# The last output tile of a fused retention and feed-forward kernel, closed one weight tile sooner and finished by column halves

## The chip, the core and the metric

The kernel runs on one core of a Trainium2 chip. The metric is the device time of one execution in microseconds (us); the kernel before takes 848.39 us, the median of 3 runs. TensorE (PE in the rows) multiplies matrices, ScalarE (ACT) and VectorE (DVE) work element by element, GpSimd (POOL) helps them, and SyncE (SP) does nothing but issue transfers. Transfers are carried by 16 DMA engines, whoever issues them; here the queues of SyncE (SPq, queue q1) and of ScalarE (ACTq, queue q10) issue.

## The reference

Eight batch entries, eight heads, 576 positions, head size 64. Retention (attention without softmax, with a decay), then a two-layer feed-forward net over the 4608 tokens:

```
scores = q @ k.T / sqrt(64)
x = (scores * decay(gamma_h, position difference >= 0)) @ v      # per batch entry and head
x = x as [4608, 512]                                             # token = 576 * batch + position
h = x @ w_in                                                     # w_in  512 x 2048
out = (h - tanh(h)) @ w_out                                      # w_out 2048 x 512
```

## The kernel before

The 576 positions are cut into nine chunks (`NC`, numbered 0 to 8) of 64 (`C`). One chunk of all eight batch entries makes a block of 512 tokens. For each block the hidden layer is made in 16 tiles (`NF`) of 128 rows, and the second product adds those 16 tiles up into four output tiles `t` of 128 tokens by 512 columns: tile `t` holds batch entries `2t` and `2t + 1`, 64 positions each. The four sums stand in four PSUM banks (`ops[n][t]`, tags o0 to o3).

Float32 is multiplied as a sum of three products of shortened words. Each hidden tile is held as a high part and a low part (`gs[n, f]`), each weight tile `wout[f]` likewise (index `a`), and the three products are high·high, high·low and low·high. So each output tile is the sum of 16 x 3 = 48 products of 128x128 by 128x512; the hidden tile is the stationary operand, which is loaded before every product, and the weight tile moves past it.

The order is written out by hand: every engine keeps the order of the program. The last block (`n` = 8, `NC - 1`) ends in one call of `mm2`, for the hidden tiles 14 and 15 together (`f - 1` and `f`). Its `groups` list says in which order (which of the two tiles, which output tile) are taken, three products each, 24 products in all. When a tile's sum is closed, `store_last` copies it out of PSUM into its quarter of one tile in SBUF (`obs[n][:, t]`): tiles 0, 2 and 3 on ScalarE (line 615), tile 1 on VectorE (line 613). Two transfers of 128 KB carry it to HBM (line 618), one for each batch entry: 64 rows of 2 KB, contiguous in HBM. The first of the two goes out on SyncE's queue and the second on ScalarE's (on SyncE's too for tile 0). Nothing follows but the end of the program (line 1322), where SyncE waits for every transfer to have landed and the engines meet.

Two more PSUM banks (tag "h", two buffers) hold scores and hidden tiles earlier on; nothing has written them since the last attention step, which is over at this point. VectorE has no more to do there than the copy of tile 1.

Of the kernel before, what the change touches and what calls it, by code (L numbers as in the profile page):

```python
# [9 lines left out]
F32 = mybir.dt.float32  # L10
# [4 lines left out]
ALU = mybir.AluOpType  # L15
# [3 lines left out]
NT, DM, DF = B * S, H * D, 2048  # L19
P = 128  # L20
NF = DF // P
NCC = DM // P
C = 64
NC = S // C
BLK = B * C
# [73 lines left out]
def retention_ffn(ctx: ExitStack, tc: tile.TileContext, ins, out, spill, wvar):  # L99
    nc = tc.nc  # L100
# [4 lines left out]
    psp = ctx.enter_context(tc.tile_pool(name="psp", bufs=1, space=PSUM))  # L105
# [6 lines left out]
    win, wout, wraw, masks = {}, {}, {}, {}  # L112
# [24 lines left out]
    halves = (slice(0, DM // 2), slice(DM // 2, DM))  # L137
# [367 lines left out]
    gs, ops, homes, obs = {}, {}, {}, {}  # L505
# [55 lines left out]
    def mm2(n, f, at=-1, between=None):  # L561
        first, final = (turn[0], turn[-1]) if n == 1 else (0, NF - 1)
        if f == first:
            ops[n] = [psp.tile([P, DM], F32, tag=f"o{t}", bufs=1, name=f"o{n}_{t}") for t in range(4)]
        if f != final:
            order = [(f, t, k) for k in range(3) for t in range(4)]
        elif n < NC - 1:
            order = [(f, t, k) for t in range(4) for k in range(3)]
        else:

            groups = [(0, 0), (0, 1), (1, 0), (1, 1), (0, 2), (1, 2), (0, 3), (1, 3)]
            order = [(f - 1 + s, t, k) for s, t in groups for k in range(3)]
        for place_, (f_, t, k) in enumerate(order):
            if place_ == at:
                between()
            g, a = [(gs[n, f_][0], 0), (gs[n, f_][0], 1), (gs[n, f_][1], 0)][k]
            nc.tensor.matmul(  # L577
                ops[n][t], g[:, t * P : (t + 1) * P], wout[f_][:, a, :],
                start=(f_ == first and k == 0), stop=(f_ == final and k == 2),
            )  # L580
            if (k, t) == (1, 2):
                middle = tc.nc.cur_bb.bb.instructions[-1].name
            if f_ == final and k == 2:
                (store_last if n == NC - 1 else store)(n, t)
        return middle

    def store(n, t):
# [150 lines left out]
    for j in range(B - 1):  # L738
# [8 lines left out]
        o = psp.tile([P, 8, C], F32, tag=("o2", "o3", "own")[j % 3], bufs=1, name=f"own_first{j}")[:, :4]  # L747
# [61 lines left out]
    first = 2 * B  # L809
# [100 lines left out]
    for k, (n, f) in enumerate(late):  # L910
        if k in (3, 16, 29):
            follow, scale = entry3(first + (0, 2, 5)[(3, 16, 29).index(k)], rest)
        if 0 < k < len(late) - 1:
            words(*late[k + 1])
        if k < len(late) - 2:
            resume(*late[k + 2])
        for ahead in (4, 5) if k == 0 else (5,):
            if k + ahead < len(late):
                fetch(*late[k + ahead])
        if k in (3, 16, 29):  # L920

            follow()
        if k in (6, 19):
            scale()
        if k in (7, 20):
            load_part(rest[0], 0)
        if k in (10, 23):
            prep(rest.pop(), 0)
        for _ in range(2 if k < 4 else 1):
            step()  # L930
        for _ in range((k > 5) + (19 < k < 26)):
            next(summed)
        if k < len(late) - 1:
            mm2(n, f)
        for _ in range({0: 3, 1: 3, 2: 3, 3: 2}.get(k, 4 < k < 16 or 21 < k < 24)):
            raw_words(*raws.pop(0))
# [258 lines left out]
    def stage_b(n, m0):  # L1195

        fetch(n, 3)
        for f in range(NF):
# [20 lines left out]
            if (n, f) != (NC - 1, NF - 2):  # L1219
                middle = mm2(n, f, later or -1, turn_)  # L1220
# [10 lines left out]
    for f in range(NF):  # L1231
        mm1(2, f)
        if f == 0:
            mm2(*late[-1])
        if f == 1:
            scale()
        for _ in range(2):
            next(summed, None)
        if f == 2:
            load_turn(2, 0)  # L1240
        if f == 6:
            prep_turn(2, 0)
            load_turn(1, 0)
            load_turn(1, 1)
        if f in (9, 10):
            prep_turn(1, f - 9)
        if 10 < f < 14:
            fetch(2, f - 11)
        if f > 13:
            split(2, f - 14, fetched.pop((2, f - 14)), False)  # L1250
# [75 lines left out]
```

## Time and profile before

| | |
|---|---|
| runs | 848.39 us (median of 847.99, 848.39, 848.69) |
| the profiled execution's own time | 849.77 us |
| its span, first to last instruction | 848.0 us |
| busy, share of the span | PE 99%, PE weight load 82%, DVE 57%, ACT 43%, POOL 10% |
| transfers | 174.95 MB, mean 206 GB/s |

The span is that of the instructions on the core; the 1.8 us between the span and the execution's own time lie around it. The busy share of TensorE includes the time in which a product drains through the array while the next one streams, so 99% says that it never stands still for long.

### The profile page before, as it was taken

The numbers are of one execution on the slowest core, as the hardware profiler recorded it, in microseconds if no ns is written. First come the engines' busy times: TensorE is split into PE (matmuls) and PEld (weight loads), VectorE is DVE, ScalarE is ACT, GpSimd is POOL, SyncE is SP. The second block draws the span as 40 slices with busy tenths as digits, with TensorE's granted clock in tenths as the row PEclk, the third lists the DMA queues.
The fourth block names the chain that finished last, engine by engine and source line by source line (L and its number), as shares of the span: only waits on it lengthen the run. The fifth ranks groups of instructions, "written<-read, shape, count | busy, mean of one in ns | idle before, by whom it ended". The sixth has DMA issues, their size and how long they took to land.

```text
span 848.0 us, 18635 instructions
## 1 busy us (share of the span) xinstructions
PE 840.1 (99%) x7694; PEld 694.0 (82%) x7694; DVE 483.4 (57%) x824; ACT 362.6 (43%) x732; POOL 82.5 (10%) x68
## 2 busy tenths in 40 slices
PE   8999999999999999999999999999999999999998
PEld 7788888888888888888888888888888888888886
DVE  5989878787567675344346755434456554443321
ACT  5887765454335454223244543322245532232321
POOL 0110002020000002111110001212100021121100
PEclk9999999999999999999999999999999999999999
DMA  9977978884787788444477665534677364452542
GB/s 342 321 293 225 371 232 300 243 280 132 224 272 271 228 308 249 149 153 170 132 236 224 209 181 194 187 125 170 207 214 209 108 201 171 133 191 75 147 115 62
DMA packets 71380, 174.95 MB, mean 206 GB/s; under 512 B 8704, under 2 KB 10368, under 8 KB 66048
## 3 DMA queue, kind: packets, MB, share of 16 engines
q1 hardware_dynamic: 70768, 172.85, 62.1%
q8 instruction: 60, 0.98, 0.5%
q10 hardware_dynamic: 528, 0.92, 0.3%
q14 instruction: 24, 0.20, 0.1%
HBM read 124.72 MB, written 48.76 MB: 205 GB/s over the span
## 4 chain that ended last, share of the span: by engine, by line
PE 97%; DVE 1%; ACT 1%; DMA 1%; issue 0%
PE o L577 32%; PE o L1136 15%; PE h L520 15%; PE pnew L1105 7%; PE pv L1105 7%; PE pown L1105 4%; PE py L1105 4%; PE pz L1105 4%; PE s L357 3%; PE new L357 2%; PE own L357 2%; DMA a<-in_first_dram 1%; PE wps L628 1%; ACT th L1155 0%; PE s_first L357 0%; PE new_first L357 0%
## 5 line engine op out<-in xcount | busy, mean ns | idle before, releaser
L577 PE MATMUL o<-wo,gh 128*128 128x512 f32 x608 | 156.0, 393 | 0.0
L577 PEld LDWEIGHTS o<-wo,gh 128*128 128x128 f32 x608 | 112.6, 188 | 24.6 <-DVE ob L599 0.4
L1159 POOL TENSOR_TENSOR c<-c,th 128x512 f32<-128x512 f32 x48 | 62.0, 1295 | 517.8 <-ACT th L1155 399.5
L1155 ACT ACTIVATE th<-c 128x512 f32<-128x512 f32 x72 | 45.5, 632 | 148.6 <-DVE c L1169 97.4
L520 PE MATMUL h<-xh,wi 128*128 128x512 f32 x384 | 98.1, 392 | 0.8 <-ACT wi L198 0.6
L520 PEld LDWEIGHTS h<-xh,wi 128*128 128x128 f32 x384 | 71.3, 188 | 17.0 <-ACT wi L198 1.1
L577 PE MATMUL o<-wo,gl 128*128 128x512 f32 x304 | 84.2, 389 | 0.0
L1136 PE MATMUL o<-wo,gs 128*128 128x512 f32 x288 | 70.6, 389 | 0.0
L577 PEld LDWEIGHTS o<-wo,gl 128*128 128x128 f32 x304 | 57.1, 188 | 11.9
L1136 PEld LDWEIGHTS o<-wo,gs 128*128 128x128 f32 x288 | 54.1, 188 | 11.2
L1105 PE MATMUL pnew<-xhv,ws 128*128 128x512 f32 x192 | 59.5, 391 | 0.3
L577 PE MATMUL o<-wo,gs 128*128 128x512 f32 x240 | 59.5, 394 | 0.0
L1105 PE MATMUL pv<-xhv,ws 128*128 128x512 f32 x192 | 59.1, 389 | 0.0
L357 PE MATMUL own<-qk,state 64*64 64x64 f32 x896 | 55.2, 221 | 0.0
L1165 DVE TENSOR_TENSOR work<-pown,work 128x512 f32<-128x512 f32 x24 | 16.6, 690 | 66.6 <-PE pown L1105 66.6
L357 PE MATMUL own<-qk,vr 64*64 64x64 f32 x928 | 54.0, 218 | 0.4 <-issue 0.4
L577 PEld LDWEIGHTS o<-wo,gs 128*128 128x128 f32 x240 | 44.4, 188 | 9.5
L520 PE MATMUL h<-xl,wi 128*128 128x512 f32 x192 | 52.1, 390 | 0.0
L1136 PE MATMUL o<-wo,gh 128*128 128x512 f32 x192 | 48.9, 389 | 0.0
L357 PEld LDWEIGHTS own<-qk,vr 64*64 64x64 f32 x928 | 45.1, 135 | 0.5 <-issue 0.5
L357 PEld LDWEIGHTS own<-qk,state 64*64 64x64 f32 x896 | 44.7, 135 | 0.0
L1121 DVE TENSOR_TENSOR gl<-s,gh 128x512 fp32r<-128x512 f32 x44 | 30.0, 688 | 23.5 <-PE o L577 13.2
(162 smaller groups left out, 1520.7 us busy)
## 6 DMA issues: line engine op xcount, KB each, us to landing
ws<-wvar_dram SPq DMA_DIRECT2D x41, 1024.0 KB, 4.9
s<-spill_dram SPq DMA_DIRECT2D x94, 256.0 KB, 4.2
qk<-in_qkv_dram SPq DMA_DIRECT2D x29, 512.0 KB, 4.8
vr<-in_qkv_dram SPq DMA_DIRECT2D x29, 512.0 KB, 4.9
spill_dram<-c SPq DMA_DIRECT2D x48, 256.0 KB, 2.6
spill_dram<-g SPq DMA_DIRECT2D x36, 256.0 KB, 3.5
rwi<-in_w_in_dram SPq DMA_DIRECT2D x16, 512.0 KB, 6.5
rwo<-in_w_out_dram SPq DMA_DIRECT2D x16, 512.0 KB, 5.4
```

The lines of the kernel that those rows point to most:

```text
L357: nc.tensor.matmul(out_, w, x, start=start, stop=stop)
L520: nc.tensor.matmul(hp, win[f][:, cc // 2, a, cc % 2 * P : (cc % 2 + 1) * P], x[:, cc, :], start=(k == 0), stop=(k == 3 * NCC - 1))
L577: nc.tensor.matmul(ops[n][t], g[:, t * P : (t + 1) * P], wout[f_][:, a, :], start=(f_ == first and k == 0), stop=(f_ == final and k == 2),)
L628: nc.tensor.matmul(wps[:, :cols], warm[:, :P], warm[:, :cols], start=True, stop=True)
L1105: nc.tensor.matmul(into, w[:, a, k], x[:, k], start=start and i == 0, stop=i == len(terms) - 1, skip_group_check=not start,)
L1121: nc.vector.tensor_tensor(gl, g, gh.bitcast(F32), op=ALU.subtract)
L1136: nc.tensor.matmul(ops[n][t], g[:, t * P : (t + 1) * P], wout[f][:, a, :], start=(j == 0 and f == fs[0] and k == 0), stop=last_,)
L1155: nc.scalar.activation(th, c, AF.Tanh)
L1159: nc.gpsimd.tensor_tensor(c, c, tanh(c), op=ALU.subtract)
L1165: nc.vector.tensor_tensor(u2, y, u2, op=ALU.add)
```

## The change

Of the last block, output tile 3 takes its products with hidden tile 14 before tile 2 takes its own, and its sum in bank o3 is closed there, one weight tile short; VectorE copies it into `obs[n][:, 3]`. The last three products of tile 3 (those with hidden tile 15) come at the very end, after tile 2 is closed and stored, in two column halves of 256, each into a bank of tag "h". VectorE adds each half to the copy in place, and each half is stored at once by a single transfer over both batch entries: the left half from SyncE's queue, the right one from ScalarE's.

```diff
-            groups = [(0, 0), (0, 1), (1, 0), (1, 1), (0, 2), (1, 2), (0, 3), (1, 3)]
+            groups = [(0, 0), (0, 1), (1, 0), (1, 1), (0, 3), (0, 2), (1, 2)]
             order = [(f - 1 + s, t, k) for s, t in groups for k in range(3)]
...
             nc.tensor.matmul(
                 ops[n][t], g[:, t * P : (t + 1) * P], wout[f_][:, a, :],
-                start=(f_ == first and k == 0), stop=(f_ == final and k == 2),
+                start=(f_ == first and k == 0), stop=(f_ == (final - 1 if n == NC - 1 and t == 3 else final) and k == 2),
             )
...
             if f_ == final and k == 2:
                 (store_last if n == NC - 1 else store)(n, t)
+            if f == final and n == NC - 1 and t == 3 and k == 2:
+                nc.vector.tensor_copy(obs[n][:, t], ops[n][t])
+        if f == final and n == NC - 1:
+            ob = obs[n][:, 3]
+            for queue, cols in zip((nc.sync, nc.scalar), halves):
+                o = psp.tile([P, BLK], F32, tag="h", bufs=2, name=f"o{n}_3_{cols.stop}")[:, : DM // 2]
+                for k, (part, a) in enumerate(((0, 0), (0, 1), (1, 0))):
+                    nc.tensor.matmul(o, gs[n, f][part][:, 3 * P :], wout[f][:, a, cols], start=(k == 0), stop=(k == 2))
+                nc.vector.tensor_tensor(ob[:, cols], o, ob[:, cols], op=ALU.add)
+                queue.dma_start(out[6:8, n * C : (n + 1) * C, cols], ob[:, cols])
```

## Rows read from the trace of the kernel before

**Rows 1.** The first page of the profile: the span, and TensorE's busy time, share of the span and instructions; and the chain of work that ended last, by engine.

```profile
span 848.0 us, 18635 instructions
PE 840.1 (99%) x7694; PEld 694.0 (82%) x7694; DVE 483.4 (57%) x824; ACT 362.6 (43%) x732; POOL 82.5 (10%) x68
...
PE 97%; DVE 1%; ACT 1%; DMA 1%; issue 0%
```

**Rows 2.** The chain that ended last, in order of time, from 820 us on: start, us, what.

```profile
819.78 24.04 PE o L577 x106
843.82 0.02 issue
843.85 0.58 ACT ob L615
```

**Rows 3.** The timeline of the end of the kernel: start us, us, engine, line, operation, out<-in, count; in brackets the idle time before and who ended it. Eight products in a row are shown first, then parts of the last 24.

```profile
835.49 1.98 PE L577 MATMUL o<-wo,gh 128*128 128x512 f32 x8
...
838.21 1.52 PE L577 MATMUL o<-wo,gs 128*128 128x512 f32 x6
...
841.13 0.69 DVE L613 COPY ob<-o 128x512 f32<-128x512 f32 x1 [4.69 <-PE o L577]
...
842.49 0.59 ACT L615 COPY ob<-o 128x512 f32<-128x512 f32 x1 [1.45 <-PE o L577]
...
843.10 0.50 ACTq L618 DMA_DIRECT2D out_dram<-ob  x1
...
843.42 0.39 PE L577 MATMUL o<-wo,gl 128*128 128x512 f32 x1
843.85 0.58 ACT L615 COPY ob<-o 128x512 f32<-128x512 f32 x1 [0.77 <-PE o L577]
844.46 0.50 ACTq L618 DMA_DIRECT2D out_dram<-ob  x1
```

**Rows 4.** The groups of instructions by line and shape, of the whole execution: count | busy us, mean ns of one | idle before. A product of 128x512, its weight load, VectorE's copy of tile 1, and an operation of VectorE on 256 columns with one operand in PSUM (`s_first`).

```profile
L577 PE MATMUL o<-wo,gl 128*128 128x512 f32 x304 | 84.2, 389 | 0.0
...
L577 PEld LDWEIGHTS o<-wo,gl 128*128 128x128 f32 x304 | 57.1, 188 | 11.9
...
L365 DVE TENSOR_TENSOR pm<-s_first,decay 128x256 f32<-128x256 f32 x7 | 2.9, 421 | 7.4 <-PE s_first L357 7.4
...
L613 DVE COPY ob<-o 128x512 f32<-128x512 f32 x1 | 0.7, 692 | 4.7 <-PE o L577 4.7
```

**Rows 5.** The issues of line 618: duration of one in ns (least, median, most), first and last start.

```profile
L618 SPq DMA_DIRECT2D out_dram<-ob x5: 466/472/597, 841.1 to 844.5; - x5
L618 ACTq DMA_DIRECT2D out_dram<-ob x3: 497/498/541, 841.9 to 844.5; - x3
```

**Rows 6.** The transfers between 838 and 848 us: packets by size (the "under" counts add up from the smallest), by queue, and issues with KB each and median us from issue to landing. These are the eight stores of the last block and nothing else.

```profile
DMA packets 640, 1.05 MB, mean 105 GB/s; under 512 B 128, under 2 KB 128, under 8 KB 640
...
q1 hardware_dynamic: 400, 0.66, 25.8%
q10 hardware_dynamic: 240, 0.39, 14.8%
...
out_dram<-ob SPq DMA_DIRECT2D x5, 128.0 KB, 2.3
out_dram<-ob ACTq DMA_DIRECT2D x3, 128.0 KB, 2.8
```

**Rows 7.** The same view of the issues between 844.44 and 844.47 us, the last two of the kernel.

```profile
out_dram<-ob SPq DMA_DIRECT2D x1, 128.0 KB, 2.3
out_dram<-ob ACTq DMA_DIRECT2D x1, 128.0 KB, 2.6
```

**Rows 8.** Stretches of the end of the kernel: busy time of the engines, then the granted clock, the mean busy share of the 16 DMA engines, and GB/s.

```profile
842.00:842.10 0.10, 0.10 (x2) 0.06 (x2) 0.00 (x0) 0.00 (x0) 0.00 (x0) 1.00 0.00 0
842.10:842.20 0.10, 0.10 (x2) 0.10 (x1) 0.00 (x0) 0.00 (x0) 0.00 (x0) 1.00 0.37 82
843.00:844.00 1.00, 0.81 (x4) 0.35 (x2) 0.00 (x0) 0.23 (x2) 0.00 (x0) 1.00 0.97 193
844.00:845.00 1.00, 0.00 (x0) 0.00 (x0) 0.00 (x0) 0.43 (x1) 0.00 (x0) 1.00 0.97 297
845.40:845.50 0.10, 0.00 (x0) 0.00 (x0) 0.00 (x0) 0.00 (x0) 0.00 (x0) 1.00 0.27 82
846.40:846.50 0.10, 0.00 (x0) 0.00 (x0) 0.00 (x0) 0.00 (x0) 0.00 (x0) 1.00 0.90 348
846.60:846.70 0.10, 0.00 (x0) 0.00 (x0) 0.00 (x0) 0.00 (x0) 0.00 (x0) 1.00 0.16 41
846.70:846.80 0.10, 0.00 (x0) 0.00 (x0) 0.00 (x0) 0.00 (x0) 0.00 (x0) 0.98 0.01 0
```

**Rows 9.** The transfers between 237.1 and 237.4 us: packets by size, and the queue with its packets, MB and share of 16 engines. In this stretch the packets are nearly all those of one load of a table (line 250), whose 128 rows are of 1 KB.

```profile
DMA packets 123, 0.12 MB, mean 396 GB/s; under 512 B 14, under 2 KB 116, under 8 KB 123
...
q1 hardware_dynamic: 123, 0.12, 126.5%
```

**Rows 10.** What SyncE's queue waited for between 835 and 849 us: us in total, times, longest.

```profile
SPq L1322 <- DMA out_dram<-ob: 1.9, 2, 1.0
```

## Prediction

> **What bounds the kernel now.** The page comes first: TensorE is busy for 99% of the span and makes 97% of the chain that ended last [rows 1]. So the body of the kernel is TensorE's, and the change takes nothing out of it: 24 products of 512 columns become 21 of 512 and 6 of 256, the same columns. What is at stake is the stretch behind the last product. The chain shows it as TensorE until 843.82, then ScalarE's copy of tile 3 until 844.43 [rows 2]; the timeline adds the two issues at 844.46 [rows 3]. There the instructions stop, but the span goes on for 3.5 us. The stretches show why: the transfers of the last tile move until 846.7 [rows 8], SyncE waits for their landing at the end of the program [rows 10], and the landing of the later one is 2.6 us after its issue [rows 7], at 847.06. The remaining 0.92 us to the end of the span, 847.98, is the closing of the program and stays. So the end is set by: last sum, copy or add, issue, transfer, landing.
>
> **The change part by part.**
>
> *Products.* Eight products take 1.98 us and one by itself 0.389 [rows 3, 4], so one follows the other after (1.98 - 0.39) / 7 = 0.227 us. The last 24 begin at 838.21 [rows 3]; number 21 begins at 842.74 and ends at 843.13, which now closes tile 2. The half products begin at 842.97. No 128x256 product of this type is in the trace. From below its pitch is half of 0.227 = 0.114; from above it is the weight load of 0.188 [rows 4], since the load is not halved. I take 0.12, near the lower end, because even with loads before each product the products of 512 columns go at their own pitch, so loads hide. The left half is then closed at 842.97 + 2 x 0.12 + 0.276 = 843.49 (at 0.188: 843.62) and the right one at 843.85 (at 0.188: 844.19). TensorE ends where it did, 843.81, or up to 0.4 later.
>
> *Copy of tile 3.* It is 0.69 us on VectorE [rows 4], from 841.82, when VectorE has finished with tile 1 [rows 3], to 842.51. VectorE has nothing else to do before 843.5, so it costs nothing; if VectorE were late, the left add would wait for it, with a reserve of 1 us. The banks "h" are free; no wait is added on TensorE.
>
> *Tile 2.* Closed by product 21 instead of 18, its copy starts 0.68 later, at 843.17 instead of 842.49 [rows 3], and its two transfers are issued at 843.78 instead of 843.10.
>
> *Adds.* 256 columns with an operand in PSUM took 0.42 [rows 4]: left 843.52 to 843.94, right 843.95 to 844.37. Before, the copy ended at 844.43. Removing that copy and adding in halves so gains 0.06.
>
> *Issues.* Queued ahead of the left half on SyncE is tile 2's first transfer, 843.78 to 844.25 (0.47 each [rows 5]); the left half is issued at 844.25. On ScalarE tile 2's second ends at 844.28, and the right half is issued at 844.40. Before, both were issued at 844.46. Gain at the later issue: 0.06 (with the slower products a loss of 0.3).
>
> *The transfers themselves.* This is the term that decides. Each store before moves 64 rows of 2 KB. The eight stores have 640 packets, of which 128 are small [rows 6]: for each store 64 of data and 16 small closing ones, one for each of 16 engines, so each engine takes four rows; the outermost count of both sides is 64. The new stores are the first of another shape: the destination `out[6:8, 64 positions, 256 columns]` counts 2 outermost, then 64 rows of 1 KB. Nothing in the trace shows how such a transfer is dealt out. One end is 16 engines, as ever; the other is that each engine takes whole steps of the outermost count, as the four rows each are consistent with, and then only two engines carry 64 KB each. I take two engines, since the dealing seen is by equal shares of an outermost count which 16 divides, and 2 can be shared by no more than two.
>
> The Trainium skill speaks against the change here ("DMA: Bandwidth & Descriptors", section "Why a DMA increments its semaphore by 16 and not by 1"): a transfer runs on the largest number of engines, up to 16, that divides the outermost count of both its sides, and on the lowest-numbered ones. By that rule these two stores run on two engines, the same two. The 16 closing packets of each store agree with it; no run here yet shows a count of 2.
>
> The price of two engines: rows of 1 KB went at 396 GB/s over 16 engines [rows 9], 24.8 GB/s on each. The slowest stretch of the stores, 193 GB/s at a busy share of 0.97 [rows 8], is 12.4 GB/s on each. I take 24.8, because two engines ask for only 50 GB/s, well under the 193 to 396 that the rows show being moved. If both halves use the same two engines, each of these carries 2 x 64 KB = 131 KB: 5.3 us at 24.8, 10.6 at 12.4. The first packet comes 1.1 us after an issue (841.06 to about 842.17 [rows 5, 8]), so from 845.35; tile 2's second store puts some 0.4 us of its own packets onto the same engines. The last data then move at 845.35 + 0.4 + 5.3 = 851.05, against 846.7 before: 4.35 us later.
>
> *Sum.* Last issue -0.06, inside the transfer's clock already; end of the data +4.35; landing and closing unchanged. Span 848.0 + 4.4 = 852.4, the execution's own time 849.77 + 4.4 = 854.2. The profiled execution is 1.4 us above the median of the runs, 848.39, so the median should be 852.8 us.
>
> **The rivals.**
>
> *Not slower: all 16 engines carry the halves.* For it: every store of the tail does so [rows 6]. Against it: none of these has a count of 2 outside. Then the right half lands 2.6 us [rows 7] after its issue at 844.40, at 847.0, a gain of 0.06. But tile 2's two transfers now fall 0.68 later onto the same engines: four transfers of 131 KB from 844.9 on. At 390 GB/s each needs 0.34 and nothing queues; at 193 each needs 0.68 and the last ends at 847.6 instead of 846.7. Between -0.1 and +0.9, with the slow products too +1.2: median 848.3 to 849.6. It decides if the new stores show 16 closing packets each.
>
> *Two engines, but not the same two.* Then each engine has 64 KB, 2.6 us, and the right half ends at 844.40 + 1.1 + 0.4 + 2.6 = 848.5: +1.8, median 850.2. Nothing in the rows tells which engines a small transfer gets.
>
> *Two engines at the slow rate.* 10.6 in place of 5.3 us: +9.7, median 858.1. The rate of 12.4 GB/s occurs only while all 16 engines write [rows 8], which speaks against it.
>
> **How the numbers follow.** 0.71 for the forecast (two engines, the same for both halves, at about the fast rate; its own range from 24.8 GB/s without tile 2's 0.4, 852.4, to 297 / 16 = 18.6 GB/s [rows 8], 7.0 us, 854.5), 0.07 for the slow rate, 0.08 for two pairs of engines, 0.14 for 16 engines. The range leaves out the last: 850.2 to 858.1. A difference under 0.2%, 1.7 us, can hardly be told from none. Sixteen engines stay within it, and so does about a third of the case of two pairs, +1.8 being next to the bound; so slower 0.83, same 0.16, faster 0.01, as no case gains more than 0.1 us.
>
> **What would show it.** Right: between 838 us and the end the six other stores have 80 packets each, and the halves 128 rows of 1 KB each with two closing packets, 740 in all, 100 of them under 512 B; the busy share of the DMA engines falls to about 2/16 = 0.12 at some 50 GB/s from 846 to 851; the halves land 5 to 7 us after their issue; SyncE's wait at the end grows by over 4 us. TensorE ends at 843.8 to 844.2, the half products start 0.12 to 0.19 apart, the adds take 0.42, the issues stand at 844.25 and 844.40. Wrong: a busy share that stays near 1 until 847 means 16 engines; a share of 0.25 means two pairs. The prediction also fails if the engines move rows of 1 KB to HBM at another rate than they loaded them from it.

## The result, and the profile after

The changed kernel takes 854.32 us (median of 6 runs, 854.05 to 854.46) against 848.23 us for the kernel before (6 runs): ratio 1.0070, 95% interval 1.0060 to 1.0081. It is 6.1 us slower. Forecast were 4.4 us more and a median of 852.8; the range of 850.2 to 858.1 holds the time.

The first page of the changed kernel, the lines that answer to [rows 1]:

```profile
span 852.6 us, 18644 instructions
PE 838.4 (98%) x7697; PEld 693.3 (81%) x7697; DVE 486.3 (57%) x827; ACT 362.2 (42%) x731; POOL 81.4 (10%) x68
```

TensorE works no longer than before; the span grew behind it. The timeline of the end, against [rows 3] and [rows 5]:

```profile
836.94 1.52 PE L577 MATMUL o<-wo,gs 128*128 128x512 f32 x6
...
840.54 0.69 DVE L586 COPY ob<-o 128x512 f32<-128x512 f32 x1
...
841.70 0.40 PE L592 MATMUL o<-wo,gh 128*128 128x256 f32 x2
...
841.93 0.28 PE L592 MATMUL o<-wo,gl 128*128 128x256 f32 x1
...
842.26 0.78 DVE L593 TENSOR_TENSOR ob<-o,ob 128x256 f32<-128x256 f32 x2 [1.02 <-PE o L592]
842.29 0.28 PE L592 MATMUL o<-wo,gl 128*128 128x256 f32 x1
842.51 0.47 SPq L628 DMA_DIRECT2D out_dram<-ob  x1
842.52 0.50 ACTq L628 DMA_DIRECT2D out_dram<-ob  x1
843.07 1.42 ACTq L594 DMA_DIRECT2D out_dram<-ob  x1
843.08 0.62 SPq L594 DMA_DIRECT2D out_dram<-ob  x1
```

This execution reached the last call 1.27 us sooner than the profiled one of before (836.94 against 838.21), before anything that the change touches. So from here on the end of a kernel is measured as a **tail**: from the start of the last call's first product to the end of the span. Before it was 847.98 - 838.21 = 9.77 us, now it is 852.58 - 836.94 = 15.64, that is 5.87 more, nearly all of the 6.1. Both halves are issued at 6.14 after the start of the tail, 0.11 sooner than tile 3 was before (844.46 - 838.21 = 6.25). All of the loss lies behind the issues.

The transfers of this stretch, against [rows 6], and what SyncE's queue waited for, against [rows 10]:

```profile
DMA packets 740, 1.05 MB, mean 70 GB/s; under 512 B 100, under 2 KB 356, under 8 KB 740
```

```profile
SPq L1332 <- DMA out_dram<-ob: 7.7, 2, 6.3
```

Six stores of 64 + 16 packets make 480; the other 260 are 2 x (128 + 2): each half has two closing packets, so two engines carried it. The wait at the end grew from 1.9 to 7.7 us. The stretches, against [rows 8] (busy times of the engines, granted clock, busy share of the DMA engines, GB/s):

```profile
844.00:845.00 1.00, 0.00 (x0) 0.00 (x0) 0.00 (x0) 0.00 (x0) 0.00 (x0) 1.00 0.63 179
845.00:846.00 1.00, 0.00 (x0) 0.00 (x0) 0.00 (x0) 0.00 (x0) 0.00 (x0) 1.00 0.10 25
846.00:847.00 1.00, 0.00 (x0) 0.00 (x0) 0.00 (x0) 0.00 (x0) 0.00 (x0) 1.00 0.14 49
847.00:848.00 1.00, 0.00 (x0) 0.00 (x0) 0.00 (x0) 0.00 (x0) 0.00 (x0) 0.53 0.13 33
848.00:849.00 1.00, 0.00 (x0) 0.00 (x0) 0.00 (x0) 0.00 (x0) 0.00 (x0) 0.50 0.14 49
849.00:850.00 1.00, 0.00 (x0) 0.00 (x0) 0.00 (x0) 0.00 (x0) 0.00 (x0) 0.50 0.14 48
850.00:851.00 1.00, 0.00 (x0) 0.00 (x0) 0.00 (x0) 0.00 (x0) 0.00 (x0) 0.50 0.13 45
851.00:852.00 1.00, 0.00 (x0) 0.00 (x0) 0.00 (x0) 0.00 (x0) 0.00 (x0) 0.50 0.02 8
```

From 845 to 851 us the busy share is 0.10 to 0.14, that is two engines of 16, and the steady rate is 49 GB/s: 24.5 on each, 42 ns for a row of 1 KB. In two of the stretches the rate falls to 25 and 33 GB/s. The granted clock falls from 1.00 to 0.50 at about 847.5 us; TensorE has made its last product at 842.57 and nothing here waits for it. By the times of the packets, the left half starts to flow at 844.82, the right one at 846.85, and the last row leaves at 851.36.

### The profile page after: what moved, and what is told of

The parts are those of the page before. It is cut to its first block, busy times and chain, and to the rows that moved or that the text cites. A ratio compares the mean times of both kernels' runs of the same rounds, so it can differ in the third digit from the quotient of the medians.

```text
span 852.6 us, 18644 instructions
## 1 busy us (share of the span) xinstructions
PE 838.4 (98%) x7697; PEld 693.3 (81%) x7697; DVE 486.3 (57%) x827; ACT 362.2 (42%) x731; POOL 81.4 (10%) x68
## 4 chain that ended last, share of the span: by engine, by line
PE 92%; DMA 3%; ACT 2%; DVE 1%; issue 0%; SPq 0%; ACTq 0%
PE o L577 29%; PE o L1146 15%; PE h L520 15%; PE pnew L1115 7%; PE pv L1115 7%; PE pown L1115 4%; PE py L1115 4%; PE pz L1115 4%; PE s L357 3%; PE new L357 2%; DMA vr<-in_qkv_dram 2%; PE own L357 2%; DMA rwi<-in_w_in_dram 1%; ACT vr L305 0%; ACT th L1165 0%
## 5 line engine op out<-in xcount | busy, mean ns | idle before, releaser
L577 PEld LDWEIGHTS o<-wo,gh 128*128 128x128 f32 x606 | 112.2, 188 | 24.5 <-DVE ob L609 0.4
```

Source lines behind the costliest of these rows:

```text
L577: nc.tensor.matmul(ops[n][t], g[:, t * P : (t + 1) * P], wout[f_][:, a, :], start=(f_ == first and k == 0), stop=(f_ == (final - 1 if n == ...
```

## The experiments

The theory was that the count of 2 outermost puts a store on two engines, the same two, and that this is the whole loss. The rivals were that the halves, the adds or the later close of tile 2 cost the time, that it is the rows of 1 KB, or that each half had engines of its own. All tails together, with the median time of each and its ratio to the kernel before on the same chip:

| kernel | first product, end of span | tail | time | ratio, 95% interval |
|---|---|---|---|---|
| before | 838.21, 847.98 | 9.77 | 848.23 | |
| changed | 836.94, 852.58 | 15.64 | 854.32 | 1.0060 to 1.0081 |
| e1_by_entry | 836.54, 846.78 | 10.24 | 848.93 | 0.9999 to 1.0016 |
| e2_shape_only | 837.33, 852.70 | 15.38 | 853.87 | 1.0049 to 1.0079 |
| e3_one_half | 837.06, 849.82 | 12.76 | 851.53 | 1.0023 to 1.0051 |
| e4_no_halves | 836.69, 846.73 | 10.04 | 848.78 | 0.9996 to 1.0014 |
| e5_one_queue | 836.65, 851.84 | 15.19 | 853.65 | 1.0050 to 1.0078 |
| e6_one_store | 837.53, 852.65 | 15.12 | 853.68 | 1.0049 to 1.0077 |
| e8_tile0_sooner | 837.10, 846.87 | 9.77 | 848.41 | 0.9989 to 1.0008 |
| e9_no_tile2_store | 837.13, 851.99 | 14.87 | 853.79, one run | |
| e10_left_half_alone | 836.94, 848.53 | 11.59 | 850.31, one run | |
| e11_two_sooner | 837.24, 846.98 | 9.74 | 848.77 | 0.9992 to 1.0011 |

**Only the shape of the stores undone.**

```diff
-            for queue, cols in zip((nc.sync, nc.scalar), halves):
+            for cols in halves:
...
-                queue.dma_start(out[6:8, n * C : (n + 1) * C, cols], ob[:, cols])
+                for u, queue in enumerate((nc.sync, nc.scalar)):
+                    queue.dma_start(out[6 + u, n * C : (n + 1) * C, cols], ob[half(u), cols])
```

> The changed kernel with one thing undone: each half is stored by two transfers, one for each batch entry, left and right half alike the first on SyncE's queue and the second on ScalarE's. Their outermost count is 64, the rows stay 1 KB. Measure of the tail: from the start of the last call's first product to the end of the span; 9.77 us before, 15.63 after the change. Theory (the count of 2 outermost puts a store on two engines, and that is the whole loss): 16 closing packets for each store, tail 9.7 to 10.4 us, time 848.1 to 848.9. Rival (the halves, the adds on VectorE and tile 2 closed 0.68 us later cost the time, or rows of 1 KB do): tail over 13 us, time over 852.

The transfers of its end:

```profile
DMA packets 800, 1.05 MB, mean 62 GB/s; under 512 B 160, under 2 KB 416, under 8 KB 800
...
out_dram<-ob ACTq DMA_DIRECT2D x2, 64.0 KB, 2.5
out_dram<-ob SPq DMA_DIRECT2D x2, 64.0 KB, 2.3
```

160 small packets are 16 for each of ten stores, so 16 engines carry each. The same 256 rows of 1 KB land 2.3 to 2.5 us after their issue, no later than the stores of before [rows 6]. The tail is 10.24 us, the time, 848.93, 0.03 above the upper edge of its window: 5.40 of the 5.87 lost are back, with halves, adds and the later tile 2 still there. The rival falls, and so does the one that rows of 1 KB are dear.

**Only the shape of the stores changed, in the kernel before.**

```diff
-            queue.dma_start(out[2 * t + u, n * C : (n + 1) * C], ob[half(u)])
+            if t == 3:
+                queue.dma_start(out[6:8, n * C : (n + 1) * C, halves[u]], ob[:, halves[u]])
+            else:
+                queue.dma_start(out[2 * t + u, n * C : (n + 1) * C], ob[half(u)])
```

> The kernel before, with its order of products and copies, and only the last two stores changed: tile 3, copied whole by ScalarE, is stored by column halves over both batch entries, 64 rows of 1 KB under a count of 2, the left half on SyncE's queue and the right one on ScalarE's. Theory (shape alone): two closing packets for each of these stores, 128 packets of 1 KB on each of two engines at 42 ns each, 5.4 us, and a late start as in the changed kernel: tail 15.2 to 15.9 us, time 853.7 to 854.5. Rival (it takes the halves and adds as well): tail under 12 us, time under 850.5.

Its transfers, and what SyncE waited for at the end:

```profile
DMA packets 740, 1.05 MB, mean 70 GB/s; under 512 B 100, under 2 KB 356, under 8 KB 740
```

```profile
SPq L1325 <- DMA out_dram<-ob: 7.4, 2, 6.6
```

The same 740 packets with 100 small ones, and 5.61 us of tail lost with every product and copy of the kernel before in its place. The shape of two stores suffices for the loss, and without it the loss is gone: that is shown from both sides.

**One half of the two on two engines.**

```diff
-                queue.dma_start(out[6:8, n * C : (n + 1) * C, cols], ob[:, cols])
+                if queue is nc.sync:
+                    for u in range(2):
+                        queue.dma_start(out[6 + u, n * C : (n + 1) * C, cols], ob[half(u), cols])
+                else:
+                    queue.dma_start(out[6:8, n * C : (n + 1) * C, cols], ob[:, cols])
```

> The changed kernel with the left half stored by batch entry (two transfers on SyncE's queue, outermost count 64) and the right half as in the change, on ScalarE's queue over both entries. Theory (same two engines for both halves, so they queue behind each other): half the work, 64 packets on each engine, 2.7 us. With the late start of the changed kernel (about 2.4 us from issue to a steady flow) the tail is 12.4 to 12.9 us and the time 850.9 to 851.4; if the start was late only because two such stores met, the data begin 1.1 us after the issue and the tail is 11.2 to 11.6 us, the time 849.7 to 850.1. Rival (each half had its own pair of engines): the tail stays at 15.6.

Its transfers:

```profile
DMA packets 770, 1.05 MB, mean 62 GB/s; under 512 B 130, under 2 KB 386, under 8 KB 770
```

130 small packets are 16 for each of eight stores and two for the right half. The tail is 12.76 us, inside the window for the same two engines with a late start; the time, 851.53, is 0.13 above its window. Taking one of the two stores off gives back 2.88 us. By estimate 2.4 of this are rows: 64 fewer on each of the two engines and 8 more, the left half's share when 16 engines carry it, 56 rows at 42 ns. The rest is about what such a store loses at its beginning (0.5 in e10 below). With a pair of its own for each half it would have given back nothing. The busy share of 0.13, not 0.25, in the changed kernel says the same.

**No halves, rows of 2 KB.**

```diff
-            for queue, cols in zip((nc.sync, nc.scalar), halves):
-                o = psp.tile([P, BLK], F32, tag="h", bufs=2, name=f"o{n}_3_{cols.stop}")[:, : DM // 2]
-                for k, (part, a) in enumerate(((0, 0), (0, 1), (1, 0))):
-                    nc.tensor.matmul(o, gs[n, f][part][:, 3 * P :], wout[f][:, a, cols], start=(k == 0), stop=(k == 2))
-                nc.vector.tensor_tensor(ob[:, cols], o, ob[:, cols], op=ALU.add)
-                queue.dma_start(out[6:8, n * C : (n + 1) * C, cols], ob[:, cols])
+            o = psp.tile([P, BLK], F32, tag="h", bufs=2, name=f"o{n}_3")
+            for k, (part, a) in enumerate(((0, 0), (0, 1), (1, 0))):
+                nc.tensor.matmul(o, gs[n, f][part][:, 3 * P :], wout[f][:, a, :], start=(k == 0), stop=(k == 2))
+            nc.vector.tensor_tensor(ob, o, ob, op=ALU.add)
+            for u, queue in enumerate((nc.sync, nc.scalar)):
+                queue.dma_start(out[6 + u, n * C : (n + 1) * C], ob[half(u)])
```

> The changed kernel without the halves: tile 3 is closed one weight tile sooner and copied as in the change, its last three products are 512 columns wide in one bank of tag h, VectorE adds the whole tile and it is stored by batch entry as before the change (rows of 2 KB, SyncE's and ScalarE's queue). Theory: the add takes 0.69 us where the copy took 0.58, tile 2's stores come 0.68 later: tail 9.8 to 10.4 us, time 848.2 to 848.9. Rival (closing tile 3 early costs by itself): time over 850.

The tail of 10.04 us is 0.27 longer than before: closing tile 3 early gains nothing. The add (0.69) takes the place of a shorter copy (0.58), which makes the issue 0.11 later. The rest comes behind the issue: the first row moves 1.36 us after it, by the packets' times, in place of 1.12 before, with tile 2's later stores just ahead of it. The time cannot be told from that of before.

**Where the flow is slow: both halves on one queue, and one store of 2 KB rows.** 131 KB at 24.5 GB/s are 5.4 us on each engine, but in the changed kernel the halves' rows move for 6.54. The first of the two kernels changes the queue in the loop:

```diff
-            for queue, cols in zip((nc.sync, nc.scalar), halves):
+            for queue, cols in zip((nc.sync, nc.sync), halves):
```

> The changed kernel with both halves issued on SyncE's queue. In the changed kernel 128 packets at 42.4 ns, 5.43 us, fill each of the two engines, but the halves' data move for 6.55 us (7.87 to 14.42 us after the tail's first product): 1.1 us are lost in two dips, where each of the two stores begins. Theory A (each store pays about 0.5 us where it begins on an engine, whichever queue it comes from): again 6.4 to 6.7 us, tail 15.4 to 15.9 us. Theory B (the second dip comes from two queues taking turns): 5.9 to 6.1 us, tail 14.9 to 15.2 us. Either way time 853.5 to 854.6.

Its stretches (columns as above):

```profile
845.00:846.00 1.00, 0.00 (x0) 0.00 (x0) 0.00 (x0) 0.00 (x0) 0.00 (x0) 0.90 0.12 38
846.00:847.00 1.00, 0.00 (x0) 0.00 (x0) 0.00 (x0) 0.00 (x0) 0.00 (x0) 0.50 0.14 48
847.00:848.00 1.00, 0.00 (x0) 0.00 (x0) 0.00 (x0) 0.00 (x0) 0.00 (x0) 0.50 0.14 48
848.00:849.00 1.00, 0.00 (x0) 0.00 (x0) 0.00 (x0) 0.00 (x0) 0.00 (x0) 0.50 0.14 48
849.00:850.00 1.00, 0.00 (x0) 0.00 (x0) 0.00 (x0) 0.00 (x0) 0.00 (x0) 0.50 0.14 48
```

The second dip is gone, and the tail is 0.45 us shorter, at the edge of the window of theory B. But the rows move for 6.26 us, which lies between the windows of both: one dip at the start remains and is larger than B had it.

The other kernel stores the whole tile at once, on top of e4:

```diff
-            for u, queue in enumerate((nc.sync, nc.scalar)):
-                queue.dma_start(out[6 + u, n * C : (n + 1) * C], ob[half(u)])
+            nc.sync.dma_start(out[6:8, n * C : (n + 1) * C], ob)
```

> The kernel of e4_no_halves (tile 3 closed early, last three products 512 wide, one add) with tile 3 stored by a single transfer over both batch entries on SyncE's queue: outermost count 2, 64 rows of 2 KB for each. Theory (two engines, each 64 packets at 80 ns, 5.1 us, and one beginning): 2 closing packets, data from 7.8 to 13.3 us after the tail's first product, tail 14.2 to 14.8 us, time 852.5 to 853.5. Rival (the loss belongs to rows of 1 KB, that is to the number of packets on an engine, 64 instead of 128): tail under 12.5 us, time under 851.

Its transfers and two of its stretches:

```profile
DMA packets 610, 1.05 MB, mean 70 GB/s; under 512 B 98, under 2 KB 98, under 8 KB 610
```

```profile
846.00:847.00 1.00, 0.00 (x0) 0.00 (x0) 0.00 (x0) 0.00 (x0) 0.00 (x0) 1.00 0.13 33
847.00:848.00 1.00, 0.00 (x0) 0.00 (x0) 0.00 (x0) 0.00 (x0) 0.00 (x0) 0.61 0.12 37
848.00:849.00 1.00, 0.00 (x0) 0.00 (x0) 0.00 (x0) 0.00 (x0) 0.00 (x0) 0.50 0.13 49
```

98 small packets are 6 x 16 + 2: the rule of the outermost count holds for rows of 2 KB too, and the number of rows on an engine is not what costs, since 64 in place of 128 give a tail of 15.12 where the two halves on one queue (e5) had 15.19. The tail missed its window by 0.3 us and the time by 0.2, for here too the flow begins slowly, at 33 to 37 GB/s in place of 49: by the packets' times the rows move for 6.1 us, where 64 rows at 80 ns are 5.1.

**Where the flow is slow: nothing ahead of the halves.** The first kernel leaves out the two stores of tile 2, so that the halves meet idle engines:

```diff
-        for u in range(2):
+        for u in range(2 if t != 2 else 0):
             queue = nc.scalar if u == 1 and t > 0 else nc.sync
```

> The changed kernel without the two stores of tile 2: that quarter of the last block is not written, so its time is read as that of a kernel with 256 KB less to store. The halves then start on idle DMA engines. Open: what makes the two stores on two engines begin slowly. Theory A (they begin while the writes of the stores ahead of them are still under way): the flow is steady from the first packet, the data move for 5.4 to 5.7 us, tail 13.4 to 13.8 us. Theory B (a store on two engines begins slowly by itself): the data move for 6.2 to 6.7 us, tail 14.2 to 14.9 us.

The second kernel leaves out the right half's store as well:

```diff
-                queue.dma_start(out[6:8, n * C : (n + 1) * C, cols], ob[:, cols])
+                if queue is nc.sync:
+                    queue.dma_start(out[6:8, n * C : (n + 1) * C, cols], ob[:, cols])
```

> As e9_no_tile2_store, and the store of the right half left out too: one store on two engines by itself, 64 packets of 1 KB on each, 2.71 us at 42.4 ns. Theory A: the data move for 2.7 to 2.9 us, tail 10.6 to 11.0 us. Theory B: 3.2 to 3.6 us, tail 11.1 to 11.7 us.

The stretches of the left half by itself:

```profile
844.00:845.00 1.00, 0.00 (x0) 0.00 (x0) 0.00 (x0) 0.00 (x0) 0.00 (x0) 1.00 0.14 37
845.00:846.00 1.00, 0.00 (x0) 0.00 (x0) 0.00 (x0) 0.00 (x0) 0.00 (x0) 1.00 0.13 36
846.00:847.00 1.00, 0.00 (x0) 0.00 (x0) 0.00 (x0) 0.00 (x0) 0.00 (x0) 0.66 0.14 48
```

Both tails, 14.87 and 11.59 us, are those of theory B. With idle engines the first row moves 1.2 us after the issue, but the rows of one half move for 3.25 us in place of 2.7, and those of both for 6.59, as in the changed kernel. So a store on two engines begins slowly by itself and loses about 0.5 us there; the writes ahead of it are not the cause. Nor is it an even crawl: in e10 most rows take 0.05 us from the start on, and 15 of the 128, all in the first 1.9 us, take 0.06 to 0.24. What holds these rows up, no run settles.

**Tile 0 sooner, in the kernel before.**

```diff
-            groups = [(0, 0), (0, 1), (1, 0), (1, 1), (0, 2), (1, 2), (0, 3), (1, 3)]
+            groups = [(0, 0), (1, 0), (0, 1), (1, 1), (0, 2), (1, 2), (0, 3), (1, 3)]
```

> The kernel before with the two first tiles of the last call closed one after the other: the groups begin (0, 0), (1, 0), (0, 1), (1, 1), so tile 0 is closed and stored 0.68 us sooner, nothing else moved. If the last stores are held up by those ahead of them (DMA engines 97% busy from 843 to 845 us before), the tail falls to 9.2 to 9.6 us; if the last product, its copy and the issue set the end, it stays at 9.7 to 9.8. Time 847.8 to 848.4 in either case.

The tail is 9.77 us, to the hundredth that of before, so nothing is to be had from storing tile 0 sooner. The trace of before speaks against a hold-up by the other tiles too: by the packets' times the first row of tile 3 moves 1.12 us after its issue (845.58 - 844.46), and the first row of tile 0, which met idle engines, took 1.13.

**The idea with the loss taken out.** Tile 3 closes with hidden tile 13 and is copied then; `groups` loses its last two entries, and the last six products of tile 3 are made in two column halves:

```diff
...
+        if f == final - 2 and n == NC - 1:
+            obs[n] = pool.tile([P, 4, DM], F32, tag="xl0", bufs=1, name=f"ob{n}")
+            nc.vector.tensor_copy(obs[n][:, 3], ops[n][3])
+        if f == final and n == NC - 1:
+            ob = obs[n][:, 3]
+            for cols in halves:
+                o = psp.tile([P, BLK], F32, tag="h", bufs=2, name=f"o{n}_3_{cols.stop}")[:, : DM // 2]
+                terms = [(f_, part, a) for f_ in (f - 1, f) for part, a in ((0, 0), (0, 1), (1, 0))]
+                for k, (f_, part, a) in enumerate(terms):
+                    nc.tensor.matmul(o, gs[n, f_][part][:, 3 * P :], wout[f_][:, a, cols], start=(k == 0), stop=(k == 5))
+                nc.vector.tensor_tensor(ob[:, cols], o, ob[:, cols], op=ALU.add)
+                for u, queue in enumerate((nc.sync, nc.scalar)):
+                    queue.dma_start(out[6 + u, n * C : (n + 1) * C, cols], ob[half(u), cols])
...
```

> The idea of the change with the loss taken out: tile 3 is closed two weight tiles sooner and copied then, tile 2 keeps its place (closed by product 18 of the last call), the last six products of tile 3 are made in two column halves in the two banks of tag h, each half is added on VectorE and stored by two transfers, one for each batch entry (outermost count 64), on SyncE's and on ScalarE's queue. If the end is set by the last add, its issue and what the DMA engines still have to move, the right half is issued 6.11 us after the tail's first product (6.25 before) and the last data end near 8.2 (8.5 before): tail 9.3 to 9.6 us against 9.77, time 0.2 to 0.5 us under that of before. If small transfers cost as much as large ones here, tail 9.8 to 10.3.

By the packets' times the last rows leave 8.24 us after the tail's first product, 0.28 sooner than before, as expected; but from there to the end of the span it takes 1.50 us in place of 1.25, and the tail, 9.74, misses its window. The time, 848.77, cannot be told from that of before. No version of the idea beats the kernel before by anything that can be measured.

## Why the prediction was right, and which term was too small

Times below are after the start of the tail (838.21 before, 836.94 after).

**Products and adds: right.** The left half was forecast closed at 5.28 and closed at 841.93 + 0.28 = 842.21, 5.27; the right one at 5.64 and at 842.57, 5.63. Two half products take 0.40 us and one 0.28, so one follows the other after 0.12, as taken: the weight loads hide. Two adds took 0.78 together. Tile 3's early copy ended at 841.23, a microsecond ahead of the first add, and cost nothing.

**Issues: right.** Forecast at 6.04 and 6.19, they came at 6.14 and 6.13, sooner than before by 0.11.

**Two engines, the same two: right.** Two closing packets for each half, a share of 0.13, 49 GB/s, and half the loss with one half (e3). The trace agrees with the rule of the Trainium skill that the prediction named ("DMA: Bandwidth & Descriptors", section "Why a DMA increments its semaphore by 16 and not by 1"): a count of 2 outermost gives 2 engines, 64 gives 16. The rate per engine was forecast as 24.8 GB/s, from a load [rows 9], and was 24.5.

**The time that the data need: too small.** The forecast was 1.1 us to the first row, 0.4 for tile 2's packets and 5.3 for the halves, the last row at 851.05 - 838.21 = 12.84. It left at 851.36 - 836.94 = 14.42, that is 1.58 later. From the last row to the end of the span it took 1.22 us, 1.25 before, so "closing unchanged" held. The halves' first row moved at 7.87, not 7.54: 0.10 of this is the later issue of the left half, and the rest lies between issue and first row, 1.74 us where 1.5 were taken. At the steady rate both halves need 5.4, 0.1 more than taken. The rest, 1.1, are the two dips: each of the two stores begins slowly. The sum had no term for that. It worked with an engine that flows from its first packet, for which the trace of before gave no row, since no engine there had more than a few packets of one of these stores. The same term made the forecast of a landing 5 to 7 us after the issue too short for the right half: the left one landed after 7.0, the right one after 851.7 - 843.1 = 8.6.

The case's own range, 852.4 to 854.5, holds the time as well, but partly by luck: its upper end stands for engines at 18.6 GB/s each, and the steady flow was at 24.5. The dips, which the range did not know of, brought the time near that end.

**The rivals.** Sixteen engines: fell at the closing packets. No run has its own case, a half in one transfer on 16 engines; the nearest, e1 with two transfers for each half, has 0.47 us more tail, inside its -0.1 to +0.9. Two pairs of engines and the slow rate of 12.4 GB/s fell with the share of 0.13 and the rate of 24.5.

## What to carry to other kernels

Before a store is widened to cover several batch entries in one transfer, look at the outermost count of its access pattern in HBM: 2 there cost 5.6 us at the end of this kernel (e2), where twice as many transfers with 64 outermost cost 0.5 us of tail and a time that cannot be told from that of before (e1). The count of small closing packets per transfer in this profile tells how many engines carried it. And where a transfer is the last thing of a kernel, forecast it from first packet to last on one engine, with a slow beginning, not from the mean rate of all 16.

## What the runs showed that was not expected

A store on two engines can also be dear to issue. On ScalarE's queue, issued with SyncE's or up to 0.4 us behind it, it took 1.08 to 1.42 us (e9, e2, e3, changed), where the two stores there in e1 took 0.56 and 0.85. On SyncE's it took 0.53 to 0.62 (e5, changed), where the stores of before took 0.47 to 0.60 [rows 5]. Such a store has 128 rows in place of 64 as well, and no run separates the two; nothing waited behind them here. The slow beginning is there with idle engines (e10: 0.5 us, e9: 1.2 for both halves), with rows of 2 KB (e6: 1.0 for the one store) and less with a second store on the same queue (e5: 0.8 for both); its cause stays open. With ten stores at the end in place of eight (e11), the closing of the program took 0.25 us longer after the last row had left, which took back what the earlier data had gained. The number of stores does not explain it by itself: e1, with ten, took 1.44 us, and e10, with five, 1.36. Why was not tried.
